# Attention scores and value products from smaller TensorE tiles: eight 64x32 tiles, four 64x64 tiles

## The chip, the cores and the metric

The kernel runs on one core of a Trainium2 chip. The core has TensorE (matrix products, written to PSUM), VectorE (DVE), ScalarE (ACT), GpSimd (POOL) and SyncE (SP, whose queue issues the transfers from and to memory). They run side by side and wait for each other through semaphores. TensorE is an array of 128 rows and 128 columns; it can be used whole or in tiles, each with its own stationary operand, and a product names the tile by the partitions that it reads and writes. Its instructions come in two rows of the profile: PE is the product, PEld the load of the stationary operand. The metric is the device time of one execution in microseconds (us).

## The reference

The inputs are `q`, `k`, `v` of shape (8 batches, 8 heads, 576, 64) and four weight matrices, all fp32. Attention is local: heads 0 to 3 see the 32 keys up to their own position, heads 4 to 7 every fourth of the last 128. Its output `x` (576 x 512 a batch) goes through a layer with sines and cosines that mixes tokens, and a channel product.

```python
scores = scale * np.matmul(q, k.transpose(0, 1, 3, 2))
mask_plain = (rel >= 0) & (rel < window)                                    # window 32
mask_dil = (rel >= 0) & (rel < window * dilation) & (rel % dilation == 0)   # dilation 4
scores = np.where(masks[None, :, :, :], scores, -1000000000.0)
attn = softmax(scores)
x = np.matmul(attn, v)            # heads side by side: (batch, 576, 512)
theta = x @ w_theta
y = w_tok_r @ (x * cos(theta)) + w_tok_i @ (x * sin(theta))
u = x + y
out = u + np.maximum(u @ w_ch, 0.0)
```

(`softmax` stands for the reference's lines with the maximum, the exponential and the sum.)

## The kernel before

**Layout.** Heads are taken in pairs, so a batch has four pairs (`NP`). On the host, the positions of the dilated heads are put in order of their residue, so that every head has a band of 32. A pair's 576 queries are 18 blocks of 32 (`QB`); each block needs 64 keys (`BW`): its own 32 and the 32 before. Nine (`NJ`) steps take two neighbouring blocks each (`e` = 0, 1).

**Scores** (`scores`, L585 to L657). The stationary operand is a block of queries of both heads, 128 rows (2 heads x 64 dimensions) by 64 columns (2 heads x 32 queries), with zeros where a head's rows meet the other's columns; the zeros are written on the host and fetched with `q`. The moving operand is 64 keys of both heads. One call gives 64 rows of scores (head, query) by 64 keys, and the calls for `e` = 0 and 1 write to PSUM partitions 0 to 63 and 64 to 127: two tiles of 128x64. A pair has 18 calls (L614), in two groups of 5 and 4 steps, each in a bank with the tag `s` (two banks). In batch 0 the mask is added by TensorE before them (`mask_on_pe`); later DVE adds it and takes the row minimum (L553), ACT takes exponentials and sums (L649), DVE the reciprocal, and POOL multiplies (L655). The result is `P`: rows (block `e`, head, query), 9 steps, 64 keys.

**The turn.** The value product needs the keys on the partitions. From batch 1 on `turn` (L659) makes eight DVE transposes a pair (L673), each of 32 partitions by 288 elements, into `pt` (two buffers), which has zeros at places that no transpose writes (`consts`, POOL memsets). In batch 0 `flip` (L691) does it on TensorE: 18 products with a unit matrix on 64x64 tiles (L709), then copies on DVE and ACT (L684, L687).

**Value products** (`pv`, L757 to L785). A call takes 128 rows of `v` (two windows of 64 keys), one head's 64 columns as stationary operand, and 64 columns of `pt` as moving one; 18 calls a pair (L773), on two tiles of 128x64, one a head. ACT copies the result to `xf` (L733); for later pairs it also restores the order of the dilated positions. `v` comes in two parts, `va` (two buffers) and `vb` (one buffer).

**What sets the order.** A class `Order` plays the program through with modelled durations (the figures behind `yield "PE"` and so on) and issues instructions in the order that this gives; ranks (`RANK`) decide between those that are ready. Batch 0, batch 1 and the first two pairs' scores of batch 2 are ordered in this way together with the preparation of the weights. From then on `phase(b)` writes out TensorE's order by hand: the token steps of batch b (`A` to `D`, L1235) with the next batch's scores and value products between them, then `th` of the next batch (L842) and the channel products `c` (L1477). Scores stand at `S_FAST = {2: 0, 3: 1, 4: 6, 5: 10}` (before that step) and value products at `PV_FAST = {0: 0, 1: 3, 2: 5, 3: 9}` (after it), in phase 1 at `S_AT` and `PV_AT`. The other engines follow by due times worked out from the plan's durations. Some channel products use the `s` banks too (`CHAN = "mmmmssxm"`, one letter a product).

**Transfers.** All are issued on SP's queue. `first_loads` (L396) fetches `q` and `k` of batch 0's four pairs, then their values. `load_qk`, `load_va` and `load_vb` fetch later pairs when a buffer comes free.

Of the kernel before, what the change touches and what calls it, by code (L numbers as in the profile page):

```python
# [20 lines left out]
QB = 32  # L21
BW = 2 * QB
NJ = S // (2 * QB)
VA = 5
NC = DM // 128
# [187 lines left out]
SLACK = 500  # L213
LATENCY = dict(PE=100.0, DVE=100.0, ACT=130.0, POOL=130.0, DMA=1800.0)
# [35 lines left out]
def build(ctx, tc, qT, kT, vw, wth, wtk, wch, maskb, ident, identb, outT):  # L250
# [60 lines left out]
    def load_qk(n):  # L311
        if n >= B * NP:
            return
        b, pr = divmod(n, NP)
        yield "rank", due.get(("scores", b, pr), od.rank)
        r = yield from take("qk", 2)
        if od.steady and b > FIRST and pr < 2:
            yield None, ("vbi", b - 1, pr + 1)
        q = ap.tile([128, 2 * NJ, 2 * QB], F32, tag="q", name=f"q{b}_{pr}")
        k = ap.tile([128, S + 32], F32, tag="k", name=f"k{b}_{pr}")  # L320
        yield "DMA", dma(2 * S)
        pin(nc.sync.dma_start(q, qT[b, pr]))
        yield "DMA", dma(S + 32)
        pin(nc.sync.dma_start(k, kT[b, pr]))
        qks[b, pr] = (q, k, r)
        signal(("qk", b, pr))
# [51 lines left out]
    KE = S + 32  # L378
# [11 lines left out]
    mskb = cp.tile([128, 6, BW], BF16, name="mskb")  # L390
# [5 lines left out]
    def first_loads():  # L396
# [3 lines left out]
        for pr in range(NP):  # L400
# [4 lines left out]
            q = q.rearrange("p a b -> p (a b)").rearrange("p (a b) -> p a b", b=2 * QB)  # L405
            k = first_k[:, KE * pr:KE * pr + KE]
            yield "DMA", dma(2 * S)
# [19 lines left out]
    def consts():  # L427
# [108 lines left out]
    def mask_of(pr, j):  # L536
        if j == 0:
            return 1
        return {2: 2, 4: 3, 6: 4, 7: 5}.get(j, 0) if pr >= NP // 2 else 0

    pmats, probs = {}, {}

    def strips():

        for hh in range(2):
            for e in range(2):
                for o in range(2):
                    yield hh, e, o
# [9 lines left out]

    def on_pe(b, pr):
        return b == 0  # L560
# [24 lines left out]
    def scores(b, pr):  # L585
        yield None, ("qk", b, pr)
        if b == 1 and on_pe(b, pr):
            yield None, "sin0"
# [11 lines left out]
        for g0, g1 in ((0, 5), (5, NJ)):  # L600
            ps, rel = yield from bank("s", f"s{b}_{pr}_{g0}")
            ps = ps[:, :(g1 - g0) * BW].rearrange("p (a b) -> p a b", b=BW)
            held[g0] = ps, rel
            if b == 2 and not od.steady:
                yield "LATER", SLACK
            masked = on_pe(b, pr)
            if masked:
                yield "PE", 150
                mask_on_pe(ps, pr, g0, g1)
            yield "PE", (148 if od.steady else 162) * (g1 - g0)  # L610
            for n in range(g0, g1):
                for e in range(2):
                    qb = 2 * n + e
                    pe(nc.tensor.matmul(ps[64 * e:64 * e + 64, n - g0], q[:, qb],  # L614
                                        k[:, QB * qb:QB * qb + BW], start=not masked, stop=not masked or n == g1 - 1))
            if masked:
                go(row_max(b, ps, rel, P, mx, g0, g1, ("mask", b, pr, g0)))
            else:
# [8 lines left out]
        if b and on_pe(b, pr):  # L627
            for g0, (ps, rel) in held.items():
                yield None, ("mask", b, pr, g0)
                yield "EXP", 335 * ps.shape[1]  # L630
                for n in range(ps.shape[1]):
                    table(nc.scalar.activation(P[:, g0 + n], ps[:, n], AF.Exp, bias=mx[:, g0 + n:g0 + n + 1],
                                               scale=SCALE, accum_out=sm[:, g0 + n, :1]))
                give(*rel)
        else:
            for g0 in (0, 5):
                yield None, ("mask", b, pr, g0)
# [5 lines left out]
        elif not on_pe(b, pr):  # L643
# [15 lines left out]
    def turn(b, pr):  # L659
# [4 lines left out]
        yield None, ("pv",) + divmod(b * NP + pr - 2, NP)  # L664
        P, rp = probs.pop((b, pr))
        pmats[b, pr] = pts[pr % 2]
        for i, (hh, e, o) in enumerate(strips()):
            if od.steady:
                yield "TURN" if i < 7 else "DVE", 482
            elif i % 2 == 0:  # L670
                yield "DVE", 940
            k0, p0 = QB * (2 * e + o), QB * (2 * e + hh)
            pin(nc.vector.transpose(pmats[b, pr][k0:k0 + QB, :, hh, QB * e:QB * e + QB],  # L673
                                    P[p0:p0 + QB, :, QB * o:QB * o + QB]))
        give("P", rp)
        signal(("pt", b, pr))

    def flip_evac(b, ps, rel, pr, g0, g1, key):
        for e in range(2):
            es, qs = slice(BW * e, BW * e + BW), slice(QB * e, QB * e + QB)  # L680
            n = (g1 - g0) * BW
            if e == 0:
                yield "DVE", dve(n)
                pin(nc.vector.tensor_copy(pmats[b, pr][es, g0:g1, :, qs], ps[es]))  # L684
            else:
                yield "ACT", act(n)
                pin(nc.scalar.copy(pmats[b, pr][es, g0:g1, :, qs], ps[es]))  # L687
        give(*rel)
        signal(key)

    def flip(b, pr):  # L691

        yield None, ("P", b, pr)
        if pr >= 1:
            yield None, ("fl", b, pr - 1)
        if b or pr >= 2:
            yield None, ("pv",) + divmod(b * NP + pr - 2, NP)
        yield None, "pts"
        pmats[b, pr] = pts[pr % 2]
        P, rp = probs.pop((b, pr))  # L700
        gs = (0, 5), (5, NJ)
        for i, (g0, g1) in enumerate(gs):
            ps, rel = yield from bank(FL0[i] if b == 0 else "xt"[i], f"pT{b}_{pr}_{g0}")
            ps = ps[:, :(g1 - g0) * BW].rearrange("p (a h b) -> p a h b", h=2, b=QB)
            yield "PE", 70 * (g1 - g0)
            for n in range(g0, g1):
                for e in range(2):
                    es = slice(BW * e, BW * e + BW)
                    pe(nc.tensor.matmul(ps[es, n - g0].rearrange("p a b -> p (a b)"), P[es, n], idt[es, es],  # L709
                                        start=True, stop=True))  # L710
            go(flip_evac(b, ps, rel, pr, g0, g1, ("fe", b, pr, g0)))
        signal(("fl", b, pr))
        for g0, _ in gs:
            yield None, ("fe", b, pr, g0)
        if b == 0:
            give(f"xh{pr}", 0)
        else:
            give("P", rp)
# [4 lines left out]
    def x_evac(b, pr, ps, rel, key):  # L723
        dst, src = xf[b, pr], ps
        if pr >= NP // 2:
            dst = dst.rearrange("p (j c) -> p c j", c=4)
            src = src.rearrange("p (c j) -> p c j", c=4)
# [29 lines left out]
    def pv(b, pr):  # L757
# [10 lines left out]
        ps = ps_v.tile([128, 2 * DM], F32, tag="v", name=f"o{b}_{pr}")[:, :S]  # L768
        yield "PE", 1060 if od.steady else 1300
        for j in range(NJ):  # L770
            v = va[:, j] if j < VA else vb[:, j - VA]
            for hh in range(2):
                pe(nc.tensor.matmul(ps[64 * hh:64 * hh + 64, BW * j:BW * j + BW], v[:, 64 * hh:64 * hh + 64],  # L773
                                    pmats[b, pr][:, j, hh], start=True, stop=True))
# [962 lines left out]
```

## Time and profile before

| what | us |
|---|---|
| median of 3 runs | 555.21 |
| lowest and highest | 554.04, 555.28 |
| the profiled execution | 555.45 |
| its span (first to last instruction) | 553.7 |

The mean granted TensorE clock of the profiled execution is 0.994 of full speed. In the profile a line names the source line (L614), the engine, and the tiles written and read (`s<-k,q`). Busy time is the time in which an engine has an instruction under way; products overlap on TensorE, so the distance between their starts says more than the duration of one. The chain of waits is followed back from the last instruction: at each step to what released it, or to the instruction before it on its engine. What lies on it sets the end; what doesn't is hidden under other work.

### The profile page before, as it was taken

What the parts mean: (1) busy time and instruction counts of PE and PEld (TensorE: products, weight loads), DVE (VectorE), ACT (ScalarE), POOL (GpSimd) and SP (SyncE); (2) the same over time, 40 slices, a digit from 0 to 9 for tenths busy, and PEclk for the clock granted to TensorE, in tenths of its full rate; (3) what the DMA queues carried; (4) which work ended last, traced back from release to release, by engine and by line L of the source; (5) the groups of instructions that cost most, each with busy time, mean ns of one, the idle gap of its engine ahead of it and who ended that gap; (6) DMA issues with size and microseconds to landing.
All of it is one profiled execution on the core that took longest, in us unless ns stands there. A gap on an engine that the chain in (4) does not pass through costs nothing.

```text
span 553.7 us, 14354 instructions
## 1 busy us (share of the span) xinstructions
PE 528.7 (95%) x5296; PEld 478.8 (86%) x5296; DVE 435.5 (79%) x1359; ACT 373.1 (67%) x1029; POOL 329.4 (59%) x347
## 2 busy tenths in 40 slices
PE   5798898999999999999999999999999999999997
PEld 4643887888899899989999899989999899989997
DVE  3878897995588797989799988989799978848322
ACT  1589977858928478768775786768776777467320
POOL 1327868899774175655468375646468365817660
PEclk9999799999999999999999999999999999999999
DMA  8985245633578938994599828993698727680722
GB/s 297 400 332 186 99 139 202 222 144 119 165 256 265 343 155 283 341 282 173 189 326 306 299 86 274 363 281 118 236 325 282 277 90 219 209 274 28 233 85 86
DMA packets 59127, 124.42 MB, mean 225 GB/s; under 512 B 5424, under 2 KB 24624, under 8 KB 58800
## 3 DMA queue, kind: packets, MB, share of 16 engines
q1 hardware_dynamic: 59056, 123.49, 65.1%
q8 instruction: 42, 0.69, 0.5%
q14 instruction: 29, 0.24, 0.1%
HBM read 99.88 MB, written 23.59 MB: 223 GB/s over the span
## 4 chain that ended last, share of the span: by engine, by line
PE 65%; DVE 10%; DMA 9%; ACT 7%; POOL 5%; issue 2%; SPq 1%; POOLq 0%; ACTq 0%; DVEq 0%
PE c L1477 15%; PE th L842 11%; PE C L1235 8%; PE A L1235 7%; PE D L1235 6%; PE o L773 5%; PE B L1235 4%; PE s L614 4%; DVE pt L673 4%; DMA va<-in_vw_dram 3%; PE y L1444 2%; PE th L824 2%; DMA xn<-xd 1%; DMA st_wtk<-in_wtk_dram 1%; DMA q<-in_qT_dram 1%
## 5 line engine op out<-in xcount | busy, mean ns | idle before, releaser
L673 DVE STREAM_TRANSPOSE pt<-P 32x288 f32<-32x288 f32 x224 | 105.1, 469 | 13.1 <-POOL P L655 8.8
L1477 PE MATMUL c<-u,late_wc 128*128 128x288 f32 x768 | 109.1, 296 | 1.2 <-DVE x L1453 1.0
L1477 PEld LDWEIGHTS c<-u,late_wc 128*128 128x128 f32 x768 | 105.5, 188 | 4.7 <-DVE x L1453 1.5
L649 ACT ACTIVATE P<-P,mx 128x64 f32<-128x64 f32 x252 | 84.4, 337 | 2.9 <-DVE mx L553 2.6
L842 PE MATMUL th<-wthh,xh 128*128 128x512 f32 x224 | 75.0, 395 | 0.2 <-DVE K L1377 0.2
L655 POOL TENSOR_TENSOR P<-P,mx 128x576 f32<-128x576 f32 x32 | 38.2, 1192 | 57.6 <-DVE mx L653 50.4
L553 DVE CUSTOM_DVE_ANT_0 P<-s,mskb 128x64 f32<-128x64 f32 x252 | 39.0, 218 | 18.0 <-PE s L614 17.7
L1251 ACT CAST u<-x 128x288 fp32r<-128x288 f32 x48 | 20.6, 430 | 45.3 <-DVE x L1261 44.8
L842 PEld LDWEIGHTS th<-wthh,xh 128*128 128x128 f32 x224 | 42.0, 188 | 9.6 <-DVE K L1377 0.4
L1253 POOL TENSOR_TENSOR u<-x,u 128x288 fp32r<-128x288 f32 x48 | 41.6, 872 | 14.4 <-ACT u L1251 14.0
L649 ACT ACTIVATION_READ_ACCUMULATOR P<-P,mx 128x1 f32 x252 | 47.3, 188 | 0.0
L842 PE MATMUL th<-wthl,xh 128*128 128x512 f32 x112 | 44.4, 396 | 0.0
L733 ACT COPY x<-o 128x576 f32<-128x576 f32 x32 | 29.4, 920 | 19.6 <-PE o L773 19.5
L489 POOL TENSOR_TENSOR zl<-g,zh 128x512 fp32r<-128x512 f32 x7 | 9.1, 1298 | 53.5 <-ACT zh L481 53.5
L614 PE MATMUL s<-k,q 128*64 128x64 f32 x1008 | 36.6, 225 | 2.7 <-DVE K L1377 2.2
L614 PEld LDWEIGHTS s<-k,q 128*64 128x64 f32 x1008 | 32.8, 139 | 7.1 <-issue 2.7
L1453 DVE SCALAR_TENSOR_TENSOR x<-c,x 128x288 f32<-128x288 f32 x64 | 28.4, 451 | 11.6 <-PE c L1477 11.4
L773 PEld LDWEIGHTS o<-pt,va 128*64 128x64 f32 x600 | 20.4, 137 | 11.7 <-DVE pt L673 3.2
L773 PE MATMUL o<-pt,va 128*64 128x64 f32 x600 | 24.8, 227 | 5.8 <-DVE pt L673 2.9
L1015 POOL TENSOR_TENSOR s<-f,x 128x256 f32<-128x256 f32 x24 | 17.8, 740 | 12.2 <-DVE f L1003 10.0
L842 PEld LDWEIGHTS th<-wthl,xh 128*128 128x128 f32 x112 | 21.0, 188 | 4.2
L1095 POOL TENSOR_TENSOR s1l<-s,s1h 128x512 fp32r<-128x512 f32 x12 | 15.4, 1288 | 14.0 <-ACT s1h L1092 14.0
(232 smaller groups left out, 1576.3 us busy)
## 6 DMA issues: line engine op xcount, KB each, us to landing
q<-in_qT_dram SPq DMA_DIRECT2D x32, 576.0 KB, 6.0
late_wt_a<-tw_t SPq DMA_DIRECT2D x24, 576.0 KB, 6.8
wt_g<-tw_b SPq DMA_DIRECT2D x22, 576.0 KB, 6.4
va<-in_vw_dram SPq DMA_DIRECT2D x30, 320.0 KB, 4.9
k<-in_kT_dram SPq DMA_DIRECT2D x28, 304.0 KB, 6.2
out_dram<-x SPq DMA_DIRECT2D x28, 288.0 KB, 2.1
vb<-in_vw_dram SPq DMA_DIRECT2D x29, 256.0 KB, 4.5
xd<-xq SPq DMA_DIRECT2D x24, 288.0 KB, 5.3
```

The source lines that it names most:

```text
L553: pin(nc.vector.tensor_tensor_reduce(out=P[:, n], in0=ps[:, n - g0], in1=mskb[:, mask_of(pr, n)], op0=ALU.add, op1=ALU.min, scale=-SCALE, ...
L614: pe(nc.tensor.matmul(ps[64 * e:64 * e + 64, n - g0], q[:, qb], k[:, QB * qb:QB * qb + BW], start=not masked, stop=not masked or n == g1 - 1))
L649: table(nc.scalar.activation(P[:, n], P[:, n], AF.Exp, bias=mx[:, n:n + 1], scale=-1.0, accum_out=sm[:, n, :1]))
L655: pin(nc.gpsimd.tensor_tensor(P, P, mx.unsqueeze(2).to_broadcast([128, NJ, BW]), op=ALU.mult))
L673: pin(nc.vector.transpose(pmats[b, pr][k0:k0 + QB, :, hh, QB * e:QB * e + QB], P[p0:p0 + QB, :, QB * o:QB * o + QB]))
L733: pin(nc.scalar.copy(dst, src))
L773: pe(nc.tensor.matmul(ps[64 * hh:64 * hh + 64, BW * j:BW * j + BW], v[:, 64 * hh:64 * hh + 64], pmats[b, pr][:, j, hh], start=True, stop=T ...
L842: pe(nc.tensor.matmul(pt, l, r, start=(n == 0), stop=(n == 3 * NC - 1)))
L1235: pe(nc.tensor.matmul(ps, l, r, start=first and n == 1, stop=last and n == 3 * len(ks), skip_group_check=more))
L1253: pin(nc.gpsimd.tensor_tensor(ul[b, d][:, ts], x[:, ts], uh[b, d][:, ts].bitcast(F32), op=ALU.subtract))
L1453: pin(nc.vector.scalar_tensor_tensor(out=x[:, ts], in0=ps, scalar=0.0, in1=x[:, ts], op0=ALU.max, op1=ALU.add))
L1477: pe(nc.tensor.matmul(ps, l[:, cs], r[:, ts], start=(n == 0), stop=(n == 3 * NC - 1)))
```

## The change

- **Scores**: the stationary operand is one head's 64 rows by 32 queries, the moving one 64 keys of that head. `block(n, e)` makes two calls, one a head (`r`), so a pair has 36 calls. Query blocks are now `n + NJ * e` (a half each) in place of `2n + e`. In the second group (steps 5 to 8) the heads change places on the host, so that the row half `r` writes to the other head's column strip. From batch 1 on the calls of both groups alternate, so that eight consecutive calls use eight different tiles and the two groups' banks. Both `s` banks are taken before the first call.
- `q` is fetched without zeros (18 x 32 columns in place of 18 x 64), `k` with 704 columns in place of 608 (four stretches with their own 32 keys ahead).
- **From batch 2 on** (`wide`), value products are 36 calls of 64x64: a half `e`'s 64 keys by one head's 64 columns, moving operand 32 queries. The eight transposes a pair stay, into `pt` without zeros.
- **In batches 0 and 1** value products are 72 calls with 32 rows and 64 columns; the two windows of 32 keys (`o`) add up in PSUM. The turn is one DVE transpose of 128 x 576. `flip` goes, in batch 0 too, and so do the memsets.
- The halves `e` of the value products are in two banks of the `v` tile, which `x_evac` reads.
- The planner's figures change: `SC_NS, PV_NS, PW_NS = 660, 1100, 600`, and in `phase` .7 for scores, .7 or 1.2 for value products in place of 1.35.
- Masks: five patterns in place of six.

```diff
+SC_NS, PV_NS, PW_NS = 660, 1100, 600
+WIDE = (0, 1, 2, 3)
+
+def wide(b, pr):
+    return b >= FIRST and pr in WIDE
...
-        q = ap.tile([128, 2 * NJ, 2 * QB], F32, tag="q", name=f"q{b}_{pr}")
-        k = ap.tile([128, S + 32], F32, tag="k", name=f"k{b}_{pr}")
+        q = ap.tile([128, 2 * NJ, QB], F32, tag="q", name=f"q{b}_{pr}")
+        k = ap.tile([128, KE], F32, tag="k", name=f"k{b}_{pr}")
...
         for n in range(2):
-            t = cp.tile([128, NJ, 2, 2 * QB], F32, name=f"pt{n}")
-            yield "POOL", 1040
-            pin(nc.gpsimd.memset(t, 0.0))
-            pts.append(t)
+            pts.append(cp.tile([128, 2 * NJ, QB], F32, name=f"pt{n}"))
...
+        groups = ((0, JS), (JS, NJ))
+
+        def block(n, e):
+            qb = n + NJ * e
+            ko = QB * (qb + 1 + 2 * e + (n >= JS)) - QB
+            for r in range(2):
+                rs, to = slice(64 * r, 64 * r + 64), QB * (2 * e + (r if n < JS else 1 - r))
+                ps = held[0 if n < JS else JS][0]
+                pe(nc.tensor.matmul(ps[to:to + QB, n % JS], q[rs, qb], k[rs, ko:ko + BW],
+                                    start=b > 0, stop=b > 0 or n in (JS - 1, NJ - 1)))
+
+        for g0, g1 in groups:
             ps, rel = yield from bank("s", f"s{b}_{pr}_{g0}")
             ps = ps[:, :(g1 - g0) * BW].rearrange("p (a b) -> p a b", b=BW)
             held[g0] = ps, rel
...
-            yield "PE", (148 if od.steady else 162) * (g1 - g0)
-            for n in range(g0, g1):
-                for e in range(2):
-                    qb = 2 * n + e
-                    pe(nc.tensor.matmul(ps[64 * e:64 * e + 64, n - g0], q[:, qb],
-                                        k[:, QB * qb:QB * qb + BW], start=not masked, stop=not masked or n == g1 - 1))
...
+            yield "PE", SC_NS
+            for i in range(JS):
+                for g0, g1 in groups:
+                    if g0 + i < g1:
+                        for e in range(2):
+                            block(g0 + i, e)
...
         pmats[b, pr] = pts[pr % 2]
-        for i, (hh, e, o) in enumerate(strips()):
...
+        if wide(b, pr):
+            pw = pmats[b, pr].rearrange("p (n h) s -> p n h s", h=2)
+            for i in range(8):
+                e, o, hh = i // 4, i // 2 % 2, i % 2
+                k0, p0 = QB * (2 * e + o), QB * (2 * e + hh)
                 yield "TURN" if i < 7 else "DVE", 482
...
+                pin(nc.vector.transpose(pw[k0:k0 + QB, :, hh], P[p0:p0 + QB, :, QB * o:QB * o + QB]))
+        else:
+            yield "DVE", 790
+            pin(nc.vector.transpose(pmats[b, pr], P.rearrange("p n (o s) -> p (n o) s", s=QB)))
...
-        dst, src = xf[b, pr], ps
+        dst, src = xf[b, pr].rearrange("p (e c) -> p e c", e=2), ps[:, :, :HS]
...
-        ps = ps_v.tile([128, 2 * DM], F32, tag="v", name=f"o{b}_{pr}")[:, :S]
-        yield "PE", 1060 if od.steady else 1300
+        ps = ps_v.tile([128, 2 * DM], F32, tag="v", name=f"o{b}_{pr}").rearrange("p (e c) -> p e c", e=2)
+        yield "PE", PW_NS if wide(b, pr) else PV_NS
         for j in range(NJ):
             v = va[:, j] if j < VA else vb[:, j - VA]
-            for hh in range(2):
-                pe(nc.tensor.matmul(ps[64 * hh:64 * hh + 64, BW * j:BW * j + BW], v[:, 64 * hh:64 * hh + 64],
-                                    pmats[b, pr][:, j, hh], start=True, stop=True))
+            if wide(b, pr):
+                for e in range(2):
+                    for hh in range(2):
+                        rs = slice(64 * e, 64 * e + 64)
+                        pe(nc.tensor.matmul(ps[64 * hh:64 * hh + 64, e, QB * j:QB * j + QB], v[rs, 64 * hh:64 * hh + 64],
+                                            pmats[b, pr][rs, 2 * j + hh], start=True, stop=True))
+                continue
+            for o in range(2):
+                for e in range(2):
+                    for hh in range(2):
+                        rs = slice(QB * (2 * e + hh), QB * (2 * e + hh) + QB)
+                        pe(nc.tensor.matmul(ps[64 * hh:64 * hh + 64, e, QB * j:QB * j + QB], v[rs, 64 * o:64 * o + 64],
+                                            pmats[b, pr][rs, 2 * j + o], start=(o == 0), stop=(o == 1)))
...
     for p in range(NP):
         go(scores(0, p), RANK["scores0"][p])
-        go(flip(0, p), RANK["flip"][p])
+        go(turn(0, p), RANK["flip"][p])
         go(pv(0, p), RANK["pv0"][p])
```

The functions `flip`, `flip_evac`, `strips` and `on_pe` are removed, and `_arrays` builds `qT`, `kT`, `vw` and the masks for the new layout.

More of the change, by code (lines that the diff above doesn't have):

```diff
@@ L389, in build @@
     idt = ids[:, :128]
-    mskb = cp.tile([128, 6, BW], BF16, name="mskb")
+    mskb = cp.tile([128, 5, BW], BF16, name="mskb")
     idb = ids[:, 128:192].bitcast(BF16)
@@ L536, in mask_of @@
     def mask_of(pr, j):
-        if j == 0:
-            return 1
-        return {2: 2, 4: 3, 6: 4, 7: 5}.get(j, 0) if pr >= NP // 2 else 0
+        if pr < NP // 2:
+            return int(j == 0)
+        return {0: 2, 4: 3, 5: 4}.get(j, 0)
     pmats, probs = {}, {}
-    def strips():
-        for hh in range(2):
-            for e in range(2):
-                for o in range(2):
-                    yield hh, e, o
     def mask_scores(ps, rel, P, mx, pr, g0, g1, key):
@@ L626, in scores @@
             go(load_qk(b * NP + pr + 2), RANK["load"][0])
[L627 to L637, printed above, removed]
+        for g0 in (0, JS):
+            yield None, ("mask", b, pr, g0)
         if b == 0:
@@ L663, in turn @@
         yield None, ("P", b, pr)
-        yield None, ("pv",) + divmod(b * NP + pr - 2, NP)
+        if b or pr >= 2:
+            yield None, ("pv",) + divmod(b * NP + pr - 2, NP)
         P, rp = probs.pop((b, pr))
         pmats[b, pr] = pts[pr % 2]
-        for i, (hh, e, o) in enumerate(strips()):
-            if od.steady:
-                yield "TURN" if i < 7 else "DVE", 482
[L670 to L715, printed above, removed]
+        if wide(b, pr):
[3 more added lines that the diff above has]
+                k0, p0 = QB * (2 * e + o), QB * (2 * e + hh)
+                yield "TURN" if i < 7 else "DVE", 482
+                pin(nc.vector.transpose(pw[k0:k0 + QB, :, hh], P[p0:p0 + QB, :, QB * o:QB * o + QB]))
+        else:
+            yield "DVE", 790
+            pin(nc.vector.transpose(pmats[b, pr], P.rearrange("p n (o s) -> p (n o) s", s=QB)))
@@ L716, in flip @@
+        if b:
+            give("P", rp)
+        else:
             give(f"xh{pr}", 0)
-        else:
-            give("P", rp)
         signal(("pt", b, pr))
@@ L1506, in phase @@
                         c, q = nb + p // NP, p % NP
-                        yield ("sc", c, q), scores(c, q), 1.35
+                        yield ("sc", c, q), scores(c, q), .7
             yield step
@@ L1511, in phase @@
                     if pv_at[p] == n:
-                        yield ("pv", nb, p), pv(nb, p), 1.35
+                        yield ("pv", nb, p), pv(nb, p), .7 if wide(nb, p) else 1.2
         rest = UNITS[8:]
@@ L1570, in steady @@
             prev = key
-            if key[0] == "sc" and not on_pe(*key[1:]):
+            if key[0] == "sc":
                 go(turn(*key[1:]), t)
@@ L1683, in _arrays @@
     q, k, v = perm(q), perm(k), perm(v)
-    qT = np.zeros((B, NP, 2, D, 2 * NJ, 2, QB), q.dtype)
-    qh = q.reshape(B, NP, 2, 2 * NJ, QB, D).transpose(0, 1, 2, 5, 3, 4)
-    for hh in range(2):
-        qT[:, :, hh, :, :, hh] = qh[:, :, hh]
-    qT = qT.reshape(B, NP, 128, 2 * NJ, 2 * QB)
-    kT = np.zeros((B, NP, 128, S + 32), k.dtype)
-    kT[..., 32:] = k.transpose(0, 1, 3, 2).reshape(B, NP, 128, S)
-    vp = np.zeros((B, H, S + 32, D), v.dtype)
-    vp[:, :, 32:] = v
-    vp = vp.reshape(B, NP, 2, S + 32, D).transpose(0, 1, 3, 2, 4).reshape(B, NP, S + 32, 128)
-    vw = np.stack([np.concatenate([vp[:, :, BW * j + QB * e:BW * j + QB * e + BW] for e in range(2)], axis=2)
-                   for j in range(NJ)], axis=3)
+    qh = q.reshape(B, NP, 2, 2, NJ, QB, D).transpose(0, 1, 2, 6, 3, 4, 5)
+    kp = np.zeros((B, NP, 2, D, S + 32), k.dtype)
+    kp[..., 32:] = k.transpose(0, 1, 3, 2).reshape(B, NP, 2, D, S)
+    vp = np.zeros((B, NP, 2, S + 32, D), v.dtype)
+    vp[..., 32:, :] = v.reshape(B, NP, 2, S, D)
+    qT = np.empty(qh.shape, q.dtype)
+    kT, at = np.empty((B, NP, 2, D, KE), k.dtype), 0
+    for e in range(2):
+        for j0, j1, flip in ((0, JS, 1), (JS, NJ, -1)):
+            qT[:, :, :, :, e, j0:j1] = qh[:, :, ::flip, :, e, j0:j1]
+            n, c0 = QB * (j1 - j0 + 1), QB * (NJ * e + j0)
+            kT[..., at:at + n] = kp[:, :, ::flip, :, c0:c0 + n]
+            at += n
+    qT = qT.reshape(B, NP, 128, 2 * NJ, QB)
+    kT = kT.reshape(B, NP, 128, KE)
+    vw = np.empty((B, NP, 2, 2, QB, NJ, 2, D), v.dtype)
+    for e in range(2):
+        for o in range(2):
+            c0 = QB * (NJ * e + o)
+            vw[:, :, e, :, :, :, o] = vp[..., c0:c0 + S // 2, :].reshape(B, NP, 2, NJ, QB, D).transpose(0, 1, 2, 4, 3, 5)
+    for b in range(B):
+        for p in range(NP):
+            if wide(b, p):
+                vw[b, p] = vw[b, p].transpose(0, 4, 2, 3, 1, 5).copy()
+    vw = vw.reshape(B, NP, 128, NJ, 128)
     wth = inp["moe_w_theta"].reshape(NC, 128, DM).transpose(1, 0, 2)
```

53 lines of the change are left out of this document (24 added, 29 removed).

## The prediction

> **What bounds the kernel now.** I read the page first (span, busy time, the shares of the chain that ended last), then the busy time by stage.
>
> ```profile
> span 553.7 us, 14354 instructions
> PE 528.7 (95%) x5296; PEld 478.8 (86%) x5296; DVE 435.5 (79%) x1359; ACT 373.1 (67%) x1029; POOL 329.4 (59%) x347
> PE 65%; DVE 10%; DMA 9%; ACT 7%; POOL 5%; issue 2%; SPq 1%; POOLq 0%; ACTq 0%; DVEq 0%
> ```
>
> ```profile
> 0.00:25.00 25.00, 16.08 (x348) 13.59 (x348) 14.35 (x41) 8.21 (x14) 5.71 (x9) 1.00 0.92 344
> 25.00:39.00 14.00, 13.55 (x127) 5.91 (x128) 10.07 (x20) 9.74 (x16) 2.63 (x2) 1.00 1.04 390
> 39.00:67.00 28.00, 23.35 (x153) 15.66 (x153) 24.90 (x70) 27.95 (x70) 22.91 (x18) 0.88 0.44 147
> 67.00:120.00 53.00, 47.85 (x540) 43.39 (x539) 47.81 (x158) 39.32 (x126) 43.35 (x43) 1.00 0.53 176
> 120.00:166.00 46.00, 44.74 (x451) 40.47 (x451) 30.74 (x104) 32.13 (x86) 38.15 (x44) 1.00 0.50 171
> 206.00:267.40 61.40, 61.40 (x634) 57.49 (x636) 55.02 (x183) 45.47 (x136) 37.40 (x41) 1.00 0.76 256
> ```
>
> The columns are stretch, length, then busy time of PE, its loads (PEld), DVE, ACT and POOL, granted clock, DMA share, GB/s. Each stage has its own limit: DMA to 25 us (share 0.92), TensorE to 39, ACT to 67 (27.95 of 28), then DVE and TensorE together to 120 (47.8 of 53 each), TensorE after that. From 206 on one batch takes 61.40 us and TensorE works in all of it, so whatever is saved on TensorE there is saved, until DVE's 55.02 is reached. The chain of waits gives the prices in that stage:
>
> ```profile
> 198.01 7.98 PE c L1477 x60
> 205.99 1.20 PE s L614 x36
> 207.19 2.58 PE A L1235 x18
> 209.77 1.20 PE o L773 x36
> 210.97 1.05 PE s L614 x36
> ...
> 218.19 3.39 PE A L1235 x24
> 221.58 1.20 PE o L773 x36
> 222.78 1.05 PE s L614 x36
> ```
>
> One head pair's scores (L614) or value products (L773) are 18 calls and 36 starts, since an fp32 call is two starts (a weight load and a product each). They take 1.05 us where the block before has the same tile shape and 1.20 where it has another, so a change of shape costs 0.15. Without it a start takes 1.05/36 = 29 ns. What sets the 29? The loads at the beginning of blocks tell:
>
> ```profile
> 28.47 0.13 PEld L824 LDWEIGHTS th<-st_wth,x 128*64 128x64 f32 x1
> 28.47 0.19 PEld L824 LDWEIGHTS th<-st_wth,x 128*64 128x64 f32 x2
> 26.65 0.30 PEld L824 LDWEIGHTS th<-st_wth,x 128*128 128x128 f32 x2
> 209.69 0.14 PEld L773 LDWEIGHTS o<-pt,va 128*64 128x64 f32 x2 [0.17 <-ACT P L649]
> 209.69 0.66 PEld L773 LDWEIGHTS o<-pt,va 128*64 128x64 f32 x20 [0.17 <-ACT P L649]
> 14.68 0.14 PEld L709 LDWEIGHTS pT<-ids,P 64*64 64x64 f32 x2 [0.21 <-POOL P L655]
> 14.68 0.66 PEld L709 LDWEIGHTS pT<-ids,P 64*64 64x64 f32 x20 [0.21 <-POOL P L655]
> L614 PEld LDWEIGHTS s<-k,q x1008: 132/138/232, 46.2 to 457.7; 128*64 128x64 f32 x168
> L842 PEld LDWEIGHTS th<-wthh,xh 128*128 128x128 f32 x224 | 42.0, 188 | 9.6 <-DVE K L1377 0.4
> ```
>
> On one tile (L824) the second 64-column load starts 0.19-0.13, about 0.055 us, after the first, and the second 128-column load 0.30-0.19, about 0.11, after: **a load takes some 0.85 ns a column, and the next load of that tile waits for it**. At the start of value products (L773, two tiles) two loads lie within 0.14, which is one load's length: they start under 10 ns apart, so on different tiles, although the code issues both starts of a call before the next tile's. Two tiles take turns together, and a round of two starts is 2 x 29 = 58 ns. A 64-column load (55) and the streaming of 64 columns for half an fp32 product fit it equally. The transposes of batch 0 (L709), on two 64*64 tiles, go at the same speed: 20 loads in 0.66, as L773's.
>
> **The change, part by part.**
>
> *Scores.* 36 calls on eight tiles, 72 starts. A stationary operand has 32 columns (27 ns by the rate above), but 64 columns still stream, so I keep 58 ns for a turn. The fifth pass uses four tiles only, so the busiest tiles have 5 calls, 10 turns: 0.58 us for 1.05, a gain of 0.47 a pair. Bounds: 72 starts at today's 29 ns are 2.1 us (1.05 worse), and nine turns with no half-empty one 0.52 (0.53 better). I take the turn, because a tile's turn is what the rows show to be kept, and the starts of two tiles lie far closer than 29 ns.
> In the steady part there are 22 such pairs (four in each of phases 1 to 5, two in phase 6): 10.3 us. But scores behind value products (16 places: three a phase, one in phase 6) now change tile shape, 0.15 each: back 2.4. **Net 7.9 us.**
> Scores now take both `s` banks before their first start. TensorE and all behind it would wait if the second were busy; in the steady phase the channel products that use these banks are followed by two others of 7.98/5 = 1.6 us each, so I cost it at nothing; uncovered it is at most half a block, 0.5 us.
>
> *Value products from batch 2 on.* 36 calls of 64x64 on four tiles: 72 starts, 18 turns, as now. The moving operand halves to 32 columns, the load keeps 64, and 64*64 tiles load as slowly as 128*64 ones (L709 rows). So a turn is still 55 to 58 ns and the block 0.99 to 1.05: **0 to 1.4 us for 24 pairs, I take 0.** If the load didn't count, a turn would be half the streaming and the same overhead, about 32 ns, and the block 0.58: 11.3 us (a rival). The eight transposes remain (DVE 469 ns each, below). The halves of `v` are fetched as before: `vb` has one buffer, its fetch is issued when the products before it end, and 3.39 us of A and half a block lie in between, all unchanged.
>
> *Batches 0 and 1.* Value products there are 72 calls of 32x64, 144 starts; only four tiles occur, as two calls add into the same output: 36 turns, 2.05 us for 1.05, **1.0 us more a pair** (bounds 1.15, if loads didn't count, and 144 x 29 ns = 4.2). For it one transpose takes the place of eight, or of TensorE's transposes with their copies:
>
> ```profile
> L673 DVE STREAM_TRANSPOSE pt<-P 32x288 f32<-32x288 f32 x224 | 105.1, 469 | 13.1 <-POOL P L655 8.8
> L897 DVE STREAM_TRANSPOSE xq<-x 128x576 f32<-128x576 f32 x24 | 17.7, 762 | 1.0 <-ACT x L733 0.9
> L684 DVE COPY pt<-pT 64x320 f32<-64x320 f32 (+1 forms) x8 | 3.6, 450 | 2.9 <-PE pT L709 2.8
> L687 ACT COPY pt<-pT 64x320 f32<-64x320 f32 (+1 forms) x8 | 3.1, 394 | 4.2 <-DVE pt L684 4.1
> 27.82 0.73 PE pT L709 x20
> ...
> 29.59 0.61 PE pT L709 x16
> ```
>
> The new one has the form of L897, 0.76 us. Batch 1: 8 x 0.469 - 0.76 = 3.0 us less DVE a pair, 12 in the stage 67 to 120, where DVE then has 36 of 53. What is late next is TensorE: 47.85 + 4 x 1.0 for value products - 6 x 0.47 for the scores of batch 1 and of two pairs of batch 2 = 49.0. So the stage can give 0 to 4 us; I take 2.5, as POOL (43.35) also has to follow. Batch 0: DVE 3.1 for 3.6, ACT 3.1 less, both under transfers, so nothing. Between 25 and 39 TensorE has two value products more by 1.0 each and loses the 36 starts of a transpose block (0.73 + 0.61 on the chain): 0.7 worse.
>
> *Transfers.*
>
> ```profile
> q<-in_qT_dram SPq DMA_DIRECT2D x32, 576.0 KB, 6.0
> k<-in_kT_dram SPq DMA_DIRECT2D x28, 304.0 KB, 6.2
> 3.07 5.78 DMA q<-in_qT_dram
> 8.87 10.37 DMA va<-in_vw_dram
> 19.32 6.10 DMA st_wtk<-in_wtk_dram
> ```
>
> `q` loses its zeros (288 KB), `k` grows from 608 to 704 columns (352 KB): 240 KB less a pair, with as many issues on SP. At the start four pairs lie ahead of the values on a queue that the chain follows to 25 us: 0.98 MB at 344 GB/s = 2.8 us sooner (0 if something else holds that stage). With the 0.7 back: 2.1. Later loads are hidden under TensorE. POOL's two memsets of `pt` go as well, off the path.
>
> The start is put in order by the kernel's own planner from its modelled durations, and these change, so an order that I don't know may cost or bring some 3 us.
>
> **Sum:** 7.9 + 0 + 2.5 + 2.1 = 12.5 us. The profiled execution took 555.45 us around its span of 553.7 (median of the runs 555.21, so it stands for them): **543 us**, alone 536 to 549 with the bounds above and the planner's 3.
>
> **The rivals.**
>
> *Loads don't hold the 64x64 tiles* (24%). For: four tiles could fetch while others stream. Against: the 55 ns between loads on one tile, and L709. Then value products gain 11.3 in the steady part; blocks of batches 0 and 1 cost 1.15 in place of 2.05, worth 1.8 before 39 us and some 2 in the stage to 120: 12.5 + 15.1, **528 us**. A batch would be 61.4 - 1.9 + 0.45 - 1.9 = 58.1, still over DVE's 55.02.
>
> *Eight tiles run no faster than four* (17%). Row halves writing to one PSUM bank could exclude each other, or a start may not pass the seven tiles before it. Scores then need 18 turns, 1.05, as now; the added shape changes cost 2.4, and the start gives 3: **555 us**, no change. Against: L709's two tiles are of different row halves and write to one bank, yet go as fast as L773's, which share their rows.
> [...]
>
> *A start has a price of its own* (9%), the slower side: with loads and streams of eight tiles overlapped, TensorE's front takes one start after another. At today's average of 29 ns, 72 starts are 2.1 us: 22 scores and 24 value products each lose 1.05 (48 us), 2.4 for shapes, the 144-start blocks of batches 0 and 1 some 13, less 4.6: **614 us**. It decides from 1.10 us a block, 15 ns a start (46 blocks then lose what the rest gains). For: nothing in the trace shows more than two starts in quick succession. Against: those two are under 10 ns apart.
> [...]
>
> **How the numbers follow.** Forecast 50%, the rivals 24, 17 and 9%. The range 525 to 556 takes in the forecast, the first rival and most of the second, and leaves out the third. About 0.3% (1.7 us) is what a measurement tells from no change. Faster by more: forecast, first rival, a third of the second, 0.79; within: 0.07; slower: the rest of the second and the third, 0.14.
>
> **What would show it.** Right: scores of 0.58 to 0.75 us in the chain with 72 starts, value products near 1.05 from batch 2 and near 2.1 before, a batch of about 60 us, the first `q` landed by 6 us. Wrong: value products of 0.6 (loads don't hold), scores of 1.05 (no eight), blocks near 1.8 to 2.1 in the steady part (price of a start), or idle TensorE between 67 and 166 us (the order at the start).

## The result, and the profile after

| | before | after |
|---|---|---|
| median of 4 runs each, us | 555.25 | 595.71 |
| lowest and highest | 554.04, 556.18 | 594.41, 614.82 |
| profiled execution, its span | 555.45, 553.7 | 595.12, 593.3 |
| first `A` step of batch 2 (end of the start) | 207.1 | 238.1 |
| first `A` step of batch 7 | 511.5 | 551.2 |

The ratio is 1.072 (95% interval 1.069 to 1.076): 40 us slower, where 12 us faster was forecast. The span grew by 39.6 us: 31.0 ahead of batch 2's first `A` step, 8.6 in the five steady batches (304.4 us became 313.0), none behind them. (The highest time of the changed kernel is a disturbed run, which the ratio leaves out.) The page of the changed kernel, span, busy times and shares of the chain:

```profile
span 593.3 us, 19775 instructions
PE 543.4 (92%) x8024; PEld 488.0 (82%) x8024; DVE 421.2 (71%) x1327; ACT 370.5 (62%) x1021; POOL 328.0 (55%) x345
PE 50%; DVE 24%; ACT 9%; issue 7%; POOL 5%; DMA 4%; SPq 1%; POOLq 0%; DVEq 0%; ACTq 0%
```

TensorE has 2728 products more, and "issue", waiting for nothing that the profile shows, went from 2% to 7%. The busy time by stage (columns as in the prediction):

```profile
0.00:25.00 25.00, 14.39 (x472) 11.56 (x475) 9.88 (x29) 3.87 (x5) 2.51 (x6) 0.83 0.92 337
25.00:39.00 14.00, 7.88 (x268) 7.50 (x264) 6.70 (x15) 1.77 (x3) 2.56 (x2) 0.50 0.68 214
39.00:67.00 28.00, 26.39 (x212) 10.85 (x212) 18.84 (x29) 22.34 (x37) 10.29 (x7) 0.92 0.34 114
67.00:120.00 53.00, 41.19 (x1119) 36.94 (x1120) 28.68 (x143) 39.56 (x133) 33.88 (x30) 0.74 0.48 143
120.00:166.00 46.00, 42.56 (x275) 38.72 (x274) 33.37 (x65) 32.86 (x73) 41.47 (x42) 1.00 0.27 93
```

From 25 to 39 us TensorE stands still almost half the time and the granted clock is 0.50; from 67 to 120 the clock is 0.74. DVE did get its time back (28.68 us for 47.81), but nobody could use it. The chain of waits in the first value products:

```profile
14.87 0.31 PE s L601 x5
15.17 0.25 PE s L563 x3
15.42 0.69 PE s L601 x40
16.11 2.10 PE o L745 x79
18.22 2.85 issue
21.07 2.02 PE o L745 x49
...
25.41 1.81 issue
27.22 3.43 PE o L745 x113
...
44.66 2.23 PE o L745 x144
```

The undisturbed block of 144 starts at 44.66 is 2.23 with its change of shape, as forecast; the first stops after 79 starts for 2.85 us. No engine and no buffer is named. The stops go with the packets of a DMA queue; its row, here before and after (packets, MB, share):

```profile
q8 instruction: 42, 0.69, 0.5%
```

```profile
q8 instruction: 63, 1.03, 0.7%
```

In the trace each packet is 16384 bytes. TensorE has 10592 loads and products before and 16048 after (with its waits for semaphores 10737 and 16189 records), and 42 and 63 packets: 255.6 and 257.0 records a packet, so I count in blocks of 256 instructions, that is 128 starts. I counted TensorE's records in the trace (loads, products and waits together, from 0) up to each place where no record begins for over 1.5 us. Nine of the changed kernel's 18 places have one position in a block of 256; here they are, with the one such place of the kernel before, from my own reading of the trace:

```
after:  begins  stands   at instruction   since the last packet began
        13.08   1.78      1*256+193       2.43 us
        17.93   3.14      2*256+193       2.45
        25.12   2.10      3*256+193       2.48
        37.22   1.93      5*256+193       2.48
       104.58   1.81     13*256+193       2.92
       113.90   1.69     15*256+193       2.46
       192.84   1.94     23*256+193       2.22
       390.00   2.25     45*256+193       2.41
       496.85   1.93     56*256+193       2.35
before: 23.75    1.59      2*256+193       2.56
packets begin, after:  12.4 18.6 24.7 30.9 36.7 43.5;  before: 16.4 22.8 29.3 36.1
```

At these places TensorE stops at instruction 193 of a block of 256 and goes on 2.22 to 2.92 us after a packet began. I take it that its program ran out; that is inferred from the positions and times, no record says it. One more stop, 3.09 us at 30.34, ends 2.51 us after a packet began too, but stands at instruction 169, and why is not known. The other eight places come before the first packet or end 8 us and more after one. In the start packets come every 5.7 to 6.8 us in both kernels; later the shortest distance is 3.4 us. An estimate from these distances: 128 starts were to be had in some 6 us there, 47 ns a start, and in 3.4 us, 26 ns a start, where packets came closest. (The 6 us is not a constant of the start: in e1 below two distances between 34 and 41 us are 3.5 and 3.3.)

### The profile page after: what moved, and what is told of

The parts are those of the page before. It is cut to its first block, busy times and chain, and to the rows that moved or that the text cites. A ratio compares the mean times of both kernels' runs of the same rounds, so it can differ in the third digit from the quotient of the medians.

```text
span 593.3 us, 19775 instructions
## 1 busy us (share of the span) xinstructions
PE 543.4 (92%) x8024; PEld 488.0 (82%) x8024; DVE 421.2 (71%) x1327; ACT 370.5 (62%) x1021; POOL 328.0 (55%) x345
## 3 DMA queue, kind: packets, MB, share of 16 engines
q8 instruction: 63, 1.03, 0.7%
## 4 chain that ended last, share of the span: by engine, by line
PE 50%; DVE 24%; ACT 9%; issue 7%; POOL 5%; DMA 4%; SPq 1%; POOLq 0%; DVEq 0%; ACTq 0%
PE c L1447 7%; DVE pt L673 7%; PE y L1414 7%; PE C L1205 6%; PE th L812 5%; PE o L745 4%; PE s L601 4%; PE D L1205 4%; PE o L738 4%; PE B L1205 3%; PE A L1205 3%; POOL P L654 2%; PE th L794 2%; DVE xh L715 2%; DVE x L892 1%
## 5 line engine op out<-in xcount | busy, mean ns | idle before, releaser
L673 DVE STREAM_TRANSPOSE pt<-P 32x288 f32<-32x288 f32 x192 | 90.1, 469 | 4.1
L812 PE MATMUL th<-wthh,xh 128*128 128x512 f32 x224 | 76.2, 401 | 4.8 <-DVE g L892 3.7
L1223 POOL TENSOR_TENSOR u<-x,u 128x288 fp32r<-128x288 f32 x48 | 40.0, 841 | 19.9 <-ACT u L1221 19.9
L601 PE MATMUL s<-k,q 64*32 64x64 f32 x2016 | 30.0, 236 | 10.2 <-issue 7.7
L1423 DVE SCALAR_TENSOR_TENSOR x<-c,x 128x288 f32<-128x288 f32 x64 | 28.6, 446 | 12.5 <-PE c L1447 12.5
L601 PEld LDWEIGHTS s<-k,q 64*32 64x32 f32 x2016 | 23.9, 111 | 14.9 <-issue 10.7
L494 POOL TENSOR_TENSOR u<-x,u 128x288 fp32r<-128x288 f32 x15 | 14.1, 939 | 21.1 <-ACT u L486 18.0
L715 DVE TENSOR_TENSOR xh<-x,xh 128x512 fp32r<-128x512 f32 x21 | 25.1, 1199 | 0.0
L1065 POOL TENSOR_TENSOR s3l<-s,s3h 128x512 fp32r<-128x512 f32 x12 | 15.5, 1289 | 14.2 <-ACT s3h L1062 14.2
```

The costliest lines, as they stand in the source:

```text
L601: pe(nc.tensor.matmul(ps[to:to + QB, n % JS], q[rs, qb], k[rs, ko:ko + BW], start=b > 0, stop=b > 0 or n in (JS - 1, NJ - 1)))
L673: pin(nc.vector.transpose(pw[k0:k0 + QB, :, hh], P[p0:p0 + QB, :, QB * o:QB * o + QB]))
L715: pin(eng.tensor_tensor(lo, x[:, :FS], hi[:, :FS].bitcast(F32), op=ALU.subtract))
L812: pe(nc.tensor.matmul(pt, l, r, start=(n == 0), stop=(n == 3 * NC - 1)))
L1223: pin(nc.gpsimd.tensor_tensor(ul[b, d][:, ts], x[:, ts], uh[b, d][:, ts].bitcast(F32), op=ALU.subtract))
```

## The experiments

**Theory A**: the instruction supply. **Theory B**: the planner's new figures put the start in a worse order. **Theory C**: in the steady part, DVE's and POOL's turns are late for the third value product. All runs come from one source with switches: `SNEW` names the batches whose scores run on eight tiles, `PVM` the value products of each batch (`o` as before, `n` 32x64, `w` 64x64), `FIG_S` and `FIG_P` whose figures the planner uses for either. The kernel before is `SNEW = (0,)*8, PVM = "o"*8`, the changed one `SNEW = (1,)*8, PVM = "nnwwwwww"`.

**e1: starts added, nothing else.**

```diff
+        for i in range({0: 108, 5: 108}.get(b, 0)):
+            r = c = i % 4
+            pe(nc.tensor.matmul(room[QB * c:QB * c + QB, i // 4:i // 4 + 1], mskb[QB * r:QB * r + QB, 0, :QB],
+                                mskb[QB * r:QB * r + QB, 0, :1], start=True, stop=True))
         for j in range(NJ):
```

> The kernel before, with 108 tiny products (bf16, 32x32 tiles, one column, into PSUM that nobody reads) ahead of each value product of batch 0 and of batch 5: 216 more TensorE instructions a block, 288 in place of 72, about as many as the changed kernel's block of 144 starts has. Nothing else differs. Theory A (instruction supply: TensorE's instructions come in blocks of 256, one every 6.1 us while the transfers of the start are busy, and TensorE stands still where it needs them sooner): the same block costs far more in batch 0 than in batch 5; batch 0's blocks take 4 to 7 us with idle time put down to issue, batch 5's 2 to 3 us; the start lengthens by 10 to 20 us, the steady batch by 3 to 6. Theory B (the loss of the start came from the planner's new figures, a start has one price everywhere): both batches' blocks grow by the same 1 to 1.6 us each, 8 to 13 us in all, spread evenly.

Measured 573.43 us, ratio 1.031 (1.024 to 1.037). The chain in batch 0 (added products L870, value products L876), then in batch 5:

```profile
33.42 0.36 PE o L870 x40
33.78 2.79 issue
36.57 0.68 PE o L870 x59
37.25 2.12 PE o L876 x36
...
347.20 0.92 PE o L870 x108
348.12 1.20 PE o L876 x36
```

The 108 products are worth 0.92 us where no stop falls in (at 347.20). In batch 0 TensorE stops for 1.4 to 2.8 us, at instruction 193 of blocks 1 to 4, three times among them, and the value products behind take 2.12 in place of 1.20. Batch 0's part cost 14.6 us (first `A` step at 221.7), batch 5's 4.4, of which four times 0.92 are the products themselves. Theory A holds, and with it comes a second cost: the clock, granted at 1.00 before from 0 to 39 us, is 0.93 and 0.65 here (0 to 25 and 25 to 39).

**e2: 64x64 value products in batches 0 and 1 too.**

```diff
-PVM = "nnwwwwww"
+PVM = "wwwwwwww"
```

> The changed kernel, with 64x64 value products (72 starts, eight transposes) in batches 0 and 1 too. Theory A: 1152 TensorE instructions fewer before 170 us, 4.5 blocks of 256; batch 0's value products come near 3.4 us where supply holds them and 1.05 where not, so the start recovers 10 to 20 us for 8 blocks that cost only 1.0 us more each by their tiles: 576 to 586 us. Theory B (planner's figures, tiles' turns): 8 x 1.05 us less on TensorE, given back in part by 12 us more DVE in batch 1: 587 to 600 us.

581.07 us, 1.043 (1.039 to 1.046), inside theory A's range: 14.6 us less than the changed kernel. The start ends at 224.1, 14.0 sooner, though DVE has its eight transposes a pair back; there is one stop at 193 ahead of 200 us, of 1.4 us, where the changed kernel's add up to 14.4. The planner's figure for these blocks changes with the edit (600 for 1100), so the order is another one too, and the 14.0 is not the starts' alone.

**e3: the kernel before with the new figures.**

```diff
-FIG_S, FIG_P = None, None
+FIG_S, FIG_P = 1, "nnwwwwww"
```

> The instructions of the kernel before, with the planner's figures of the changed one (scores 660 ns, value products 1100 and 600, 0.7 and 1.2 in the plan of the steady part). Theory A: 552 to 561 us, the start within 3 us of before, no idle time of TensorE put down to issue beyond before's. Theory B: most of the 31 us that the start lost are here too, 575 to 590 us. Theory C for the steady part (the other engines' due times, moved by the plan's shorter durations, make the third value product of a batch late): a batch takes 62.5 to 65 us in place of 61.4 here too.

572.32 us, 1.027 (1.023 to 1.030): 15.6 us lost with the same instructions in another order, which is between the theories. The start ends at 219.5, 12.4 later. TensorE's timeline there:

```profile
90.18 0.56 PE L1562 MATMUL y<-late_wt_b,z 128*128 128x288 f32 x3
91.11 0.33 PE L877 MATMUL o<-pt,va 128*64 128x64 f32 x2 [0.37 <-ACT x L830]
99.22 1.22 PE L877 MATMUL o<-pt,va 128*64 128x64 f32 x17 [7.79 <-DVE pt L751]
```

The planner, which thinks the value product cheap and early, queued it ahead of other token products; it waits 7.79 us for DVE's transposes. The clock is 0.70 between 90 and 107 us. Batches are 61.8 to 62.3 us: theory C's direction, but short of its 62.5.

**e4 and e12: scores alone, in all batches, with new and with old figures.**

```diff
-SNEW = (0,)*8
+SNEW = (1,)*8      # e12 with FIG_S = 0
```

> The kernel before, with only the scores changed, in all batches: 36 calls on eight 64x32 tiles, no zeros in q; blocks paired as before, value products, turns and masks as before. Theory A: 72 more instructions a block, in the start 8 blocks with 576 more, 2.3 blocks of 256, of which batch 0's 288 come at 6.1 us a 256: 4 to 9 us later; in the steady part 0.30 us less a block less shape changes, 5 to 8 us back; in all 551 to 560. If scores on eight tiles are what makes the steady batch longer than 61.4 us (theory C: both groups end at once and the turn chain on DVE and POOL gets no earlier), a batch takes 62 to 64 here; if the 64x64 value products do it, 60.2 to 61.

> The kernel with the scores alone changed, in all batches, with the planner's figures of the kernel before. With the new figures the start was 12.5 us late, and only 2.0 us of that were stalls at instruction 193 of a block. Theory B (the order of the start): the old figures bring back 6 to 12 us of it, 556 to 563 us. Theory A alone (the added starts): the start stays 10 to 13 us late, 564 to 568, with the steady part 0.6 us a batch better.

e4: 569.06 us, 1.022 (1.019 to 1.026), above theory A's range; the start ends 12.5 later with only 2.0 us of stops at 193, a batch takes 61.7 to 63.6. e12: 562.95, 1.012 (1.009 to 1.015); the start is still 9.4 late, with 4.1 us of stops, and a batch takes 60.7 to 61.2. So the figures explain the batch and 3 us of the start (6 to 12 were expected). The other 9 I can't divide between supply, clock and order: e12's start isn't ordered as before's either, as scores now end both groups at once.

**e5: the changed kernel with the old figures.**

```diff
-FIG_S, FIG_P = None, None
+FIG_S, FIG_P = 0, "oooooooo"
```

> The instructions of the changed kernel, with the planner's figures of the kernel before (scores 148 to 162 ns a step, value products 1060 or 1300, 1.35 in the plan). Theory B (figures): the 12 us that the figures alone cost the start of the old instructions come back, and with them 0.5 us a batch of the steady part: 578 to 586 us. Theory A (supply): batch 0's value products still take 5 to 7 us in place of 2.08, with TensorE idle on issue; the start stays 12 to 22 us behind before's. Theory C (the steady batch is longer because of the new tiles themselves): a batch still takes 62.5 to 65 us; if the due times made it longer, 60.5 to 62.

582.49 us, 1.046 (1.040 to 1.052). The start ends at 224.7: 13.4 sooner than the changed kernel's, close to the 12.4 that the same figures cost in e3, and 17.6 later than before's. Stops at 193 remain, 14 us of them ahead of 200 us. So B and A both hold. The first four batches take 61.1 to 64.2, which fits neither half of what was expected of theory C; stops at 193 lie in these batches too (8 us in all behind 200 us).

**e8: only the value products and turns of batches 0 and 1.**

```diff
-PVM = "oooooooo"
+PVM = "nnoooooo"
```

> The kernel before, with only the value products and turns of batches 0 and 1 changed (72 calls of 32x64, 144 starts a pair, one DVE transpose, no transposes on TensorE; rows of these batches in another order), old figures in the plan. Theory A: batch 0 has 288 instructions a pair in place of 72 + 72 of the block and its transposes, 576 more in all, 2.25 blocks of 256 at 6.1 us: its blocks take 4 to 7 us, the start is 10 to 16 us later; steady part 61.4 a batch: 565 to 573 us. Theory B (supply doesn't matter, only the tiles' turns at 2.08 and the order): blocks of 2.08, the start within 4 us of before: 552 to 560.

576.51 us, 1.035 (1.030 to 1.040): worse than both theories. Batch 0 stops at 193 for 1.6, 3.1, 1.7 and 2.1 us, as A says; but the start ends 23.3 later, more than the 14.0 that e2 gives for these blocks. Its order is another one as well (the turns moved to DVE), so A's size is not shown by this run. Nor do the parts add up: with the old figures these blocks alone cost the start 23.3 us and the scores alone 9.4 (e12), and e5, which has both, lost 17.6.

**e6: scores alone, from batch 3 on.**

```diff
-SNEW = (0,)*8
+SNEW = (0, 0, 0, 1, 1, 1, 1, 1)    # FIG_S = 0
```

> The kernel before up to batch 2, instruction for instruction; from batch 3 on only the scores changed (36 calls on eight tiles, no zeros in q), with the old figures in the plan. By the prices of the blocks (0.76 and a change of shape 0.15 each, in place of 1.00 to 1.05) a batch is 0.7 us shorter, 60.7: 3.5 us in all, 551 to 553 us. If scores of both groups at once hold up the turns or the `s` banks, a batch is 61.4 to 62.5 and the time 555 to 560.

**552.00 us, 0.992 (0.989 to 0.995)**: faster than both kernels. Four batches:

```profile
207.20:267.90 60.70, 60.70 (x782) 56.48 (x777) 53.52 (x184) 46.51 (x135) 37.46 (x42) 1.00 0.72 243
267.90:328.50 60.60, 60.60 (x778) 56.41 (x776) 52.44 (x180) 44.61 (x134) 35.52 (x40) 1.00 0.71 237
328.50:389.20 60.70, 60.70 (x783) 56.45 (x777) 52.52 (x180) 45.15 (x134) 36.05 (x40) 1.00 0.72 238
389.20:449.90 60.70, 60.70 (x780) 56.48 (x777) 52.51 (x180) 44.92 (x134) 35.81 (x40) 1.00 0.71 237
```

TensorE works all the time, and a batch is 0.7 us shorter, which is what the blocks' prices give (four of 0.90 in the chain, for 1.20 and three of 1.05: 0.75). One of the four:

```profile
209.85 1.20 PE o L877 x36
211.05 0.90 PE s L662 x58
211.95 2.58 PE B L1353 x18
```

(The chain gives 58 of the block's 72 starts to it; the others begin while the value products still run.)

**e11: the same with the new figures.**

```diff
-FIG_S = 0
+FIG_S = None       # 660 ns and .7 from batch 3 on
```

> The kernel with the scores alone changed from batch 3 on, but with the changed kernel's figures for them (660 ns, 0.7 in the plan) from batch 3 on. The instructions of TensorE are the same and in the same order; only the due times of the other engines' work move. Theory C (in the steady part the plan's shorter durations make DVE's turns late): a batch takes 61.2 to 62.2 us in place of 60.67, the third value product of a batch 1.2 to 1.5 us in place of 1.05; 554 to 559 us. If the figures don't matter there: 60.7 and 552.

559.01 us, 1.005 (1.003 to 1.007). Same instructions on TensorE, other due times for the rest:

```profile
271.70:333.80 62.10, 61.44 (x787) 56.71 (x776) 53.92 (x180) 45.49 (x133) 35.57 (x41) 1.00 0.71 232
```

```profile
286.44 1.46 PE o L876 x36
```

The third value product takes 1.46 with its change of shape in place of 1.20, and a first `A` step waits for DVE. The figures alone cost 1.4 us a batch, twice what the blocks bring. Theory C holds, and the due times are its cause, not the tiles.

**e7, e9, e10: both new blocks from batch 3 on, alone and with 33 or 66 tiny products ahead** (rows in another order in all three).

```diff
-PVM = "oooooooo"   # e6
+PVM = "ooowwwww"   # e7; e9 and e10: 33 and 66 of e1's products ahead of the last value product of batch 2
```

> As the run with the scores from batch 3 on, with 64x64 value products from batch 3 on as well (their rows come out in another order; nothing else is left out). By the prices of the blocks (1.18 in place of 1.20) the same 551 to 553 us as there. If the 64x64 products hold something up (the third of a batch took 1.51 in the changed kernel), some 0.3 to 0.5 us a batch more, 552.5 to 555.5.

> The kernel with both new blocks from batch 3 on, with 33 tiny products (66 TensorE instructions, bf16, one column, read by nobody) put ahead of the last value product of batch 2, at 168 us. Everything behind them is the same work in the same order. In the run without them the four steady batches from 208 us on took 67.3, 60.6, 64.1 and 64.7 us; their first A step is instruction 79, 145, 209 and 19 of its block of 256, as a batch has 7 x 256 + 66. Theory A (supply: TensorE stands still where it comes to instruction 193 of a block inside a dense stretch): the 66 instructions move each batch to the next one's place, so the lengths move up by one: about 60.6, 64, 64.7 and then that of place 84 or so (61 to 67). The first batch is 4 to 7 us shorter although 33 products were added. Rival (the stalls belong to what that batch's transfers and other engines do): the lengths stay 67.3, 60.6, 64.1, 64.7, and the time grows by 0.2 to 0.4 us.

> The same with 66 tiny products (132 instructions). Theory A: the lengths move up by two places: about 64, 64.7, 61 to 67, and 60.6 to 61 for the last (place 151, near 145). Rival: 67.3, 60.6, 64.1, 64.7 as without them.

e7: 567.11 us, 1.019 (1.015 to 1.022), a miss by 12 us. Batches of e7, e9 and e10:

```profile
208.50:275.80 67.30, 62.96 (x922) 58.52 (x920) 53.73 (x184) 46.66 (x135) 37.35 (x42) 0.95 0.67 219
275.80:336.40 60.60, 60.60 (x926) 56.47 (x920) 52.40 (x180) 44.69 (x134) 35.56 (x40) 1.00 0.72 238
336.40:400.50 64.10, 62.14 (x925) 57.78 (x920) 52.72 (x180) 45.21 (x134) 36.32 (x40) 0.97 0.69 230
400.50:465.20 64.70, 62.48 (x925) 57.92 (x921) 52.73 (x180) 44.93 (x133) 35.88 (x39) 0.97 0.68 223
```

```profile
209.00:270.10 61.10, 60.76 (x928) 56.49 (x920) 53.66 (x184) 46.38 (x135) 37.40 (x42) 1.00 0.72 241
270.10:333.30 63.20, 60.96 (x925) 56.61 (x920) 52.80 (x180) 45.18 (x134) 35.63 (x40) 1.00 0.71 232
333.30:398.20 64.90, 62.41 (x925) 57.84 (x920) 52.74 (x180) 44.96 (x133) 35.86 (x39) 0.97 0.69 223
398.20:464.50 66.30, 62.69 (x927) 58.19 (x921) 52.72 (x180) 45.02 (x133) 35.69 (x39) 0.97 0.66 214
```

```profile
209.80:274.10 64.30, 62.15 (x925) 57.83 (x920) 52.74 (x180) 45.33 (x134) 36.37 (x40) 0.97 0.70 229
274.10:338.60 64.50, 62.26 (x926) 57.98 (x920) 52.75 (x180) 44.88 (x133) 35.85 (x39) 0.97 0.68 224
338.60:405.60 67.00, 63.08 (x926) 58.62 (x921) 52.70 (x180) 45.03 (x133) 35.68 (x39) 0.95 0.65 212
405.60:466.40 60.80, 60.80 (x923) 56.50 (x920) 52.61 (x180) 44.96 (x134) 35.87 (x40) 1.00 0.72 238
```

In order of the place of a batch's first `A` step in its block of 256 instructions:

```
place     79    145   210/211   19..21   84..86   150/151
e7       67.3   60.6    64.1     64.7
e9              61.1    63.2     64.9     66.3
e10                     64.3     64.5     67.0     60.8
```

The length of a batch goes with its place in the blocks of 256 and hardly with anything else: 33 useless products make the first steady batch 6.2 us shorter and the last of the four 1.6 longer. That is the order which theory A expected; lengths that belong to the batches, the rival, would have stayed 67.3, 60.6, 64.1 and 64.7. A stop, in e7's chain:

```profile
360.16 1.18 PE o L884 x72
361.34 0.77 PE s L662 x52
362.11 1.96 issue
364.07 0.44 PE s L662 x10
```

Value products and scores stand side by side at three places of a batch, 288 instructions in about 2 us. The timeline has 72 starts of value products and 62 of scores ahead of this stop, 268 instructions, so two marks (instruction 193 of two blocks) fall into the pair, and TensorE stands 1.96 us at the second. In e6 such a pair has 216, and TensorE is busy in all of the four batches (60.70 us of 60.70 in the first). e9 and e10 as a whole took 565.23 and 565.91 us (1.018 and 1.017): the losses move, their sum hardly changes.

## Why the prediction was wrong, step by step

- **What bounds the kernel**: right; e6 shows that time saved on TensorE in the steady part is saved.
- **Scores on eight tiles**: 72 starts take 0.76 us, not 0.58, a gain of 0.24 to 0.29 a pair in place of 0.47. With the shape changes a batch gains 0.7 us in place of 1.4. The mechanism was right for the first 32 starts: in e6's block at 222.7 the trace has them eight at a time, 7 ns apart, a turn every 56 ns (the first 80). The other 40 come 12 ns apart on average, and what holds them the runs don't show.
- **64x64 value products**: 1.03 us, in 0.99 to 1.05. The rival *loads don't hold* falls.
- **32x64 value products**: 2.08 us undisturbed, for 2.05. **Here the sum failed**: "1.0 us more a pair" priced the block by its tiles, and nothing by its 288 instructions. In the start, where packets began 5.7 to 6.8 us apart, TensorE stopped in three of batch 0's four for 1.9 to 3.1 us, and the granted clock was 0.50 from 25 to 39 us. e2 takes them out, with the order that follows, and gets 14.0 us of the start back.
- **The turn of batch 1, 2.5 us**: DVE's time in the stage 67 to 120 fell by more than the 12 us forecast, but no run shows a gain from it.
- **The planner's order, "some 3 us"**: 12.4 (e3) and 13.4 us (e5) in the start, four times the bound; 1.4 us a batch in the steady part (e11), where I counted nothing. Taken one after the other from the changed kernel, the figures are 13.4 of the 31.0 us lost in the start (e5) and the 32x64 blocks 14.0 (e2). This is no division of the 31.0: e8 and e12 show that such parts don't add up.
- **The steady part** as a whole: 8.6 us lost in five batches. An estimate from the runs: the blocks bring 0.8 a batch (4), the figures cost 1.4 (7), and four stops at 193 stand 6.2 us; together 9.
- **Transfers**: the first scores began at 5.76 us in place of 6.7, as expected, but the start was not bound there any more.
- *Eight tiles run no faster than four*: falls, 0.76 us for 1.05. Both row halves wrote to one bank of scores, in different partitions, and were not slowed to 1.05.
- *A start has a price of its own* (9%): the sign came true, and the size of the loss nearly, but the mechanism is another, so the size is luck. Inside a block without a stop 72 starts take 0.76 us, 10.5 ns each, so TensorE's front doesn't hold them to 29. In the steady part such blocks take 0.76 and 1.03 us, not 2.1, and no run shows the 1.8 us with which the prediction's mark for this rival begins. What the runs show in its place is the estimate above, 26 to 47 ns a start, paid for 128 starts together where they came faster than packets did.

The profile of before held the sign: a stop of 1.59 us at 23.75, and packets every 6.4 to 6.8 us in the start. I didn't read the instruction queue's row.

## What to carry to other kernels

Count TensorE's instructions as traffic: before cutting blocks into smaller tiles, compare the number of starts in each dense stretch with what the instruction queue delivers in it (here 128 starts a packet, packets 5.7 to 6.8 us apart in the start, 3.4 at the closest later). Keep planner figures that were tuned to an order when you shorten blocks, or change them in a run of their own: here they cost 1.4 us a batch (e11), and the blocks brought 0.7 (e6). A change that pays in the steady part can be put there alone (e6, 552.00 us), away from a start that is full.

## What the runs showed of the hardware

- In the kernels before and after, one packet of the queue `q8 instruction` goes with some 256 of TensorE's instructions (42 packets for 10737 records, 63 for 16189). Of the ten stops of over 1.5 us in the changed kernel that end within 3 us of the start of a packet, nine are at instruction 193 of a block of 256; there TensorE went on 2.2 to 2.9 us after the packet began.
- Packets came little ahead of their use. In none of the 14 traces did packet n (from 0) begin before TensorE had started instruction 151 of block n (the earliest is 159 in the kernel before and 154 in the changed one), and in none did TensorE pass instruction 193 of block n + 1 sooner than 2.2 us after that packet began (2.52 and 2.22). An estimate from these: no more than 256 + 193 - 151 = 298 instructions lay ready. A pair of blocks with 288 was stopped in e7 (1.96 us at 362.11); pairs with 216 were not in e6.
- After stops of 1.4 to 2.8 us the clock was halved: in e1 for 3.4, 6.8 and 6.8 us after those at 193, and for 10.2 us after another wait of 2.2 us at 68 (the granted clock there is 0.93 to 25 us, 0.65 to 39, 0.93 to 67 and 0.88 to 110). It does not always follow: in the changed kernel it stayed whole after the stops at 192.84 and 496.85 in the table (1.00 from 180 to 210 and from 450 to 550 us). That the stops cause it is inferred: in e1 only the starts were added.
- Why packets are slower in the start (5.7 to 6.8 us apart; transfers busy 0.92 of the time to 25 us, 0.68 from there to 39 in the changed kernel) was not tried by itself.
